# Gathering the first mixture's tokens in quarter rows, turning them on VectorE, and reading the newest activations last in its second products

## The chip, the cores and the metric

The kernel runs on one core of one Trainium2 chip. The metric is the device time of one execution in microseconds, the median of several runs. The engines are TensorE (PE; its weight loads are listed apart as PEld), VectorE (DVE), ScalarE (ACT), GpSimd (POOL) and SyncE (SP, which issues loads). Each works through its own instructions in order and waits for the others by semaphores.

## The reference

Three stages follow each other, all in float32. The first is a retention: per head a state that decays by gamma and takes in k times v, read by q. Its output is written as 1536 token rows of 512. The second is a mixture with hard routing: each token goes to the expert with the largest of 8 logits. The third is a mixture in which all 4 experts see every token, weighted by given probabilities.

```python
logits = x @ w_gate                       # first mixture: N=1536, D=512, E=8, F=1024
expert_idx = np.argmax(logits, axis=1)
# token i takes the next free place of its expert (capacity N // E * 2 = 384)
h = np.maximum(np.einsum('ecd,edf->ecf', disp, w1), 0.0)
y = np.einsum('ecf,efd->ecd', h, w2)
out[i] = gate_w[i] * y[expert_idx[i], pos[i]]
...
for e in range(E):                        # second mixture: E=4, F=1024
    h = np.maximum(x @ w1[e], 0.0)
    out += p[:, e:e + 1] * (h @ w2[e])
```

## The kernel before

**Precision.** A float32 matrix is split into a rounded high part and the remaining low part; a product is hi*hi + hi*lo + lo*hi. In the first mixture `pair` does this with two matmuls: the weights' high part against the tokens' high and low part side by side (448 columns), then the weights' low part against the tokens' high part (224). Splitting costs one ScalarE cast (L124) and one VectorE subtraction (L125) per weight unit of 128x1024 (`split_w`). The units of expert e are 8e to 8e+7: four for its first product (w1), four for its second (w2). SP loads a unit (L111) into one of four buffers, which is free again when the VectorE subtraction of an earlier unit has read it. `upto(u)` says how far the splits run ahead of the unit in use.

**Retention stage.** Twelve tiles of 128 tokens pass through matmuls; POOL scales v (`vg`, L230) and the outputs (`xT`, L316). `x_pe` turns a tile into token rows, ScalarE copies them to `xk` (L363), and an ACT-queue transfer writes them to `xd` in memory. VectorE works out each token's expert and rank, and matmuls collect into `slot_ps` which token stands at which place of which expert. `gidx` (L543) is the list of token numbers for 256 places of 8 experts. Expert 0's tokens are collected already transposed, by matmuls into `xt0` (`late`, `fetched`, L499 and L507), and split into `xet[0]` (L713, L717). Then all engines pass a branch (`overflow`, L580 and L581) that is not taken with these inputs.

**First mixture.** For each expert e: four groups c of the first product (L860, L863 with `xet`), each ending with ScalarE copy and Relu (L887, L888) and VectorE sum and low part (L889, L890) that give two of the eight blocks `hs`; then the tokens of expert e+1 are prepared by `prep_x`; then four output blocks d of the second product (L860, L863 with `h`), of which each two are summed into `x2` (L921, L922). `prep_x(e+1)` transposes the gathered rows with 8 TensorE matmuls against an identity (L701), splits them (L707, L708) and starts the gather for expert e+3 (`load_xe`, L570): two POOL instructions, each of 128 whole rows. Up to 224 places of an expert are used (`SM`). In between VectorE works off `tables` (pieces of the scatter tables), POOL scatters them (`scatter`, L841), and `combine_w` prepares weights for the second mixture.

**Second mixture.** All the rest, from `first_pair` on; it is TensorE's products nearly without a gap.

The order on each engine is the order in the code (the schedule is manual). What orders the preparation for the next expert is this end of the first product and the loop behind it:

```python
        if e + 1 < E1:
            prep_x(e + 1)
        if e == 3:
            for _ in pieces:
                pass
```

Of the kernel before, what the change touches and what calls it, by code (L numbers as in the profile page):

```python
# [37 lines left out]
NS = 2 * E2 * 4  # L38

C_D = 0  # L40
C_GK = C_D + P
C_IW = C_GK + NCH * 8
# [13 lines left out]
def tile_retention_moe_moe(ctx: ExitStack, tc, qkv, cst, gqt, a1, a2, b1, b2, out, cap):  # L56
# [31 lines left out]
    raws = {}  # L88
    ws = {}
# [10 lines left out]
    def wsrc(u):  # L100
        if isinstance(u, int):
            e, c = divmod(u, 8)
            return (a1 if c < 4 else a2)[e, c % 4]
        kind, n = u
        return (b1 if kind == "p" else b2)[n // 4 % E2, n % 4]
# [47 lines left out]
    gidx0 = pc.tile([P, SL // P], I32, name="gidx0")  # L153
    gidx = pc.tile([P, SL // P, E1], I32, name="gidx")
# [19 lines left out]
    pc.tile([P, 32], F32, name="edge")  # L174

    with ExitStack() as actx:
# [8 lines left out]
        zero = pa.tile([1, D], F32, name="zero")  # L185
        causal = cdec[:, C_D:C_GK].rearrange("p (o t) -> p o t", o=1).to_broadcast([P, 4, P])
        gk = cdec[:, C_GK:C_IW].rearrange("p (c h) -> p c h", c=NCH)
# [166 lines left out]
        def x_reduce(i):  # L354
            bks, part = xbs.pop(i)
            xk = xks[i]
            for g in range(2):
# [6 lines left out]
                    xk[:, g * 256:(g + 1) * 256].rearrange("p (q c) -> p q c", q=2), b3[:, :, 0:P]  # L364
# [72 lines left out]
        for it in range(NT):  # L437
# [105 lines left out]
        nc.vector.tensor_copy(gidx, slot_ps)  # L543
# [35 lines left out]
    def overflow():  # L579
        some = nc.values_load(nbi[0:1, 8:9], min_val=0, max_val=NB)  # L580
        with tc.If(some > 0, preferred_fallthrough_block=False), tc.tile_pool(name="pg", bufs=1, side="right") as pg:  # L581
# [23 lines left out]
            with tc.For_i(0, E1, 1) as e:  # L605
# [14 lines left out]
                with tc.For_i(0, blocks, 1) as j:  # L620
# [9 lines left out]
                    )  # L630
                    bk = bank("gt")
                    for k in range(KD):
                        nc.tensor.transpose(
                            bk[:, k * P:(k + 1) * P], xg[:, k * P:(k + 1) * P], ident
# [41 lines left out]
    xet = {}  # L676
    xet[0] = pw.tile([P, 2, 1024], F32R, tag="w", name="xet0").rearrange(
        "p a (b s t) -> p (a b) s t", b=2, s=2
    )[:, :, :, 0:SM]
# [12 lines left out]
    def prep_x(e):  # L692
        t = xe.pop(e)
        r = pe.tile([P, KD, 2, SL], F32R, tag="xet", name=f"xet{e}")[:, :, :, 0:SM]
        xet[e] = r
        t2 = duo(f"T{e}")
        bks = [t2[:, g] for g in range(2)]
        for b in range(2):
            for g in range(2):
                for q in range(2):  # L700
                    nc.tensor.transpose(  # L701
                        bks[g][:, (2 * q + b) * P:(2 * q + b + 1) * P],
                        t[:, b, (2 * g + q) * P:(2 * g + q + 1) * P], ident,
                    )
        t4 = t2.rearrange("p g (q t) -> p g q t", q=2)[:, :, :, 0:SM]
        hi, lo = (r[:, :, n].rearrange("p (g q) t -> p g q t", g=2) for n in range(2))
        nc.scalar.copy(hi, t4)  # L707
        nc.vector.tensor_tensor(out=lo, in0=t4, in1=hi.bitcast(F32), op=ALU.subtract)  # L708
# [3 lines left out]
    def hi0(g):  # L712
        nc.scalar.copy(xet[0][:, 2 * g:2 * g + 2, 0], xt0[g])  # L713

    def lo0(g):
        x = xet[0][:, 2 * g:2 * g + 2]
        nc.vector.tensor_tensor(  # L717
            out=x[:, :, 1], in0=xt0[g], in1=x[:, :, 0].bitcast(F32), op=ALU.subtract
        )

    hi0(0)
    lo0(0)
    hi0(1)
    lo0(1)
# [113 lines left out]

    def scatter(some):
# [28 lines left out]
    for e in range(E1):  # L868
        x = xet.pop(e)
        hs = []  # L870
        for c in range(4):
# [23 lines left out]
            if c != 2:  # L895
                upto(u)
# [408 lines left out]
```

## Time and profile before

| | |
|---|---|
| median of 3 runs | 744.47 us (744.29 to 746.27) |
| the profiled execution's own time | 744.18 us |
| its span, from first to last instruction | 742.4 us |
| mean granted TensorE clock | 0.997 |
| busy PE / PEld / DVE / ACT / POOL | 727.5 / 661.8 / 469.0 / 338.8 / 167.6 us |
| first mixture's first product to the second mixture's first | 68.13 to 237.22 us |

Times in the rows below are microseconds from the span's start unless marked ns. In a row of the time line the first number is the start and the second the length; "x8" is eight instructions shown as one row; a bracket at the end is the idle time of the engine ahead of the row and what ended it. Matmuls overlap: a new one starts before the last has ended, so their spacing counts, not their length.

### The profile page before, as it was taken

The numbers are of one execution on the slowest core, as the hardware profiler recorded it, in microseconds if no ns is written. First come the engines' busy times: TensorE is split into PE (matmuls) and PEld (weight loads), VectorE is DVE, ScalarE is ACT, GpSimd is POOL, SyncE is SP. The second block draws the span as 40 slices with busy tenths as digits, with TensorE's granted clock in tenths as the row PEclk, the third lists the DMA queues.
The fourth block names the chain that finished last, engine by engine and source line by source line (L and its number), as shares of the span: only waits on it lengthen the run. The fifth ranks groups of instructions, "written<-read, shape, count | busy, mean of one in ns | idle before, by whom it ended". The sixth has DMA issues, their size and how long they took to land.

```text
span 742.4 us, 11359 instructions
## 1 busy us (share of the span) xinstructions
PE 727.5 (98%) x4466; PEld 661.8 (89%) x4467; DVE 469.0 (63%) x769; ACT 338.8 (46%) x545; POOL 167.6 (23%) x158
## 2 busy tenths in 40 slices
PE   8998999999999999999999999999999999999996
PEld 5887999999998888899988999889998899988895
DVE  4888889887887935634754645773375454557334
ACT  2334666675665624334443335633445334453341
POOL 3543111222310011222222211213421121111103
PEclk9999999999999999999999999999999999999998
DMA  9985876687561122211113122112221212112002
GB/s 336 409 325 160 298 259 217 214 277 240 201 200 57 40 75 64 103 61 57 57 60 100 41 85 86 58 62 95 100 72 72 86 56 86 58 57 86 29 0 86
DMA packets 27642, 93.22 MB, mean 126 GB/s; under 512 B 3617, under 2 KB 3889, under 8 KB 27586
## 3 DMA queue, kind: packets, MB, share of 16 engines
q1 hardware_dynamic: 23042, 81.79, 31.9%
q0 software_dynamic: 2672, 7.44, 3.2%
q10 hardware_dynamic: 1872, 3.24, 1.1%
q8 instruction: 36, 0.59, 0.3%
q14 instruction: 20, 0.16, 0.1%
HBM read 86.11 MB, written 6.34 MB: 125 GB/s over the span
## 4 chain that ended last, share of the span: by engine, by line
PE 85%; DVE 5%; DMA 5%; ACT 1%; issue 1%; POOL 1%; POOLq 0%; SPq 0%; ACTq 0%; DVEq 0%
PE o L1111 35%; PE a L955 17%; PE m L860 11%; PE b L955 8%; PE m L863 5%; PE bb L955 5%; DMA kv<-qkv 2%; DVE w L125 2%; DMA qk<-qkv 1%; DMA xd<-xk 1%; DVE tsum L889 1%; PE O L301 1%; PE S L246 1%; DMA raw<-a 1%; PE T L701 1%
## 5 line engine op out<-in xcount | busy, mean ns | idle before, releaser
L1111 PE MATMUL o<-w,g_c 128*128 128x512 f32 x1152 | 267.4, 390 | 0.0
L1111 PEld LDWEIGHTS o<-w,g_c 128*128 128x128 f32 x1152 | 215.8, 188 | 43.8
L125 DVE TENSOR_TENSOR w<-raw,w 128x1024 fp32r<-128x1024 f32 x128 | 158.2, 1245 | 16.9 <-ACT w L124 16.7
L955 PE MATMUL a<-X,w 128*128 128x384 f32 x720 | 145.1, 336 | 0.0
L124 ACT CAST w<-raw 128x1024 fp32r<-128x1024 f32 x128 | 132.6, 1048 | 5.9 <-DMA raw<-a 4.2
L990 DVE TENSOR_TENSOR c<-b,c 128x384 f32<-128x384 f32 x30 | 16.7, 558 | 181.2 <-PE b L955 181.2
L955 PEld LDWEIGHTS a<-X,w 128*128 128x128 f32 x720 | 127.3, 188 | 2.6 <-DVE c L990 0.3
L139 POOL TENSOR_TENSOR t<-raw 128x512 f32<-128x512 f32 x28 | 38.8, 1386 | 375.2 <-DMA raw<-b 326.9
L986 ACT COPY c<-a 128x384 f32<-128x384 f32 x60 | 28.7, 479 | 196.4 <-PE a L955 196.4
L860 PE MATMUL m<-h,w 128*128 128x448 f32 x256 | 81.7, 378 | 1.7 <-DVE h L890 1.7
L860 PE MATMUL m<-xet,w 128*128 128x448 f32 x256 | 80.8, 375 | 0.9 <-DVE xet L717 0.9
L971 ACT ACTIVATE g_c<-c 128x384 fp32r<-128x384 f32 x96 | 50.4, 526 | 66.2 <-DVE c L990 64.9
L955 PE MATMUL b<-X,w 128*128 128x384 f32 x360 | 72.0, 334 | 0.0
L863 PE MATMUL m<-h,w 128*128 128x224 f32 x256 | 67.4, 263 | 0.0
L863 PE MATMUL m<-xet,w 128*128 128x224 f32 x256 | 67.4, 263 | 0.0
L955 PEld LDWEIGHTS b<-X,w 128*128 128x128 f32 x360 | 63.5, 188 | 0.0
L975 DVE SCALAR_TENSOR_TENSOR g_c<-c,g_c 128x384 fp32r<-128x384 f32 x96 | 52.9, 552 | 4.0
L860 PEld LDWEIGHTS m<-h,w 128*128 128x128 f32 x256 | 48.0, 187 | 6.1 <-ACT w L124 2.2
L860 PEld LDWEIGHTS m<-xet,w 128*128 128x128 f32 x256 | 48.0, 187 | 4.7 <-PEq L581 1.0
L863 PEld LDWEIGHTS m<-h,w 128*128 128x128 f32 x256 | 48.8, 191 | 0.0
L863 PEld LDWEIGHTS m<-xet,w 128*128 128x128 f32 x256 | 48.8, 190 | 0.0
L955 PE MATMUL bb<-X,w 128*128 128x384 f32 x204 | 41.3, 339 | 0.1
(148 smaller groups left out, 747.1 us busy)
## 6 DMA issues: line engine op xcount, KB each, us to landing
raw<-a SPq DMA_DIRECT2D x64, 512.0 KB, 4.3
raw<-b SPq DMA_DIRECT2D x64, 512.0 KB, 3.5
qk<-qkv SPq DMA_DIRECT2D x12, 512.0 KB, 8.4
kv<-qkv SPq DMA_DIRECT2D x12, 512.0 KB, 8.3
xd<-xk ACTq DMA_DIRECT2D x12, 256.0 KB, 6.6
gqs<-gqt SPq DMA_DIRECT2D x6, 256.0 KB, 7.7
iw<-cst SPq DMA_DIRECT2D x1, 272.0 KB
xe<-xd,gidx POOLq DMA_INDIRECT x16, 4.2
```

Source lines behind the costliest of these rows:

```text
L124: nc.scalar.copy(w[:, 0], r)
L125: nc.vector.tensor_tensor(out=w[:, 1], in0=r, in1=w[:, 0].bitcast(F32), op=ALU.subtract)
L139: eng.tensor_tensor(out=c[:, 0:2], in0=b[:, 2:4], in1=b[:, 1:3], op=sub)
L246: nc.tensor.matmul(out=bks[j][:, cols], lhsT=qk[r, 1, cols], rhs=qk[r, 0, cols], start=True, stop=True,)
L860: nc.tensor.matmul(out=b2, lhsT=w[0], rhs=x, start=first, stop=last, skip_group_check=True)
L863: nc.tensor.matmul(out=b2[:, 0], lhsT=w[1], rhs=x[:, 0], start=False, stop=last, skip_group_check=True)
L955: nc.tensor.matmul(out=bk[:, 0:HT], lhsT=w[:, sw, k], rhs=x[:, sx, k], start=(first and m == 0), stop=(m == len(steps) - 1), skip_group_ch ...
L971: nc.scalar.activation(out=h2[:, 0], in_=src, func=AF.Relu)
L975: nc.vector.scalar_tensor_tensor(out=h2[:, 1], in0=src, scalar=0.0, in1=h2[:, 0].bitcast(F32), op0=ALU.max, op1=ALU.subtract,)
L986: nc.scalar.copy(t, bk[:, 0:HT])
L990: nc.vector.tensor_tensor(out=t, in0=bk[:, 0:HT], in1=t, op=ALU.add)
L1111: nc.tensor.matmul(out=bk, lhsT=h2[:, sh, cols], rhs=w[:, sw, k], start=(q == 0 and m == 0 and (n, t) not in begun), stop=(m == 2), skip_g ...
```

## The change

The tokens of experts 1 to 7 are gathered in quarter rows. `xd` is read as four times as many rows of 128 floats, and one gather instruction fetches 32 tokens with their four quarters, one quarter to each group of 32 partitions. So an expert takes 7 gather instructions (224 / 32) where it took 2. The rows of `xd` are stored with their columns permuted, so that VectorE's transpose of 32x32 squares (one instruction, `turn_x`) gives the transposed tokens; the 8 TensorE transposes are gone. The index list is made by repeating each token number four times over partitions with seven small matmuls against `rep` (filled by POOL in the third retention tile), times four plus the quarter's number (`gidx`, now one VectorE instruction from PSUM). Expert 0's tokens, which are not gathered this way, keep the permuted column order, and its w1 comes in that order as a separate input `a0`.

The order of work: `turn_x(e+1)` stands in the third group (c = 2) of expert e, the high part behind the fourth group, the low part behind the second product's first pair of output blocks. For expert 1 the turn stands in expert 0's d = 1, the high part behind that place's splits, and the low part behind the split in d = 2. `xet[0]` is made ahead of the overflow branch, and `gidx` behind it but also ahead of the branch. Output blocks d = 0 and 1 are issued together: six of the eight steps of each, then the four steps that read the two newest blocks of h. Some splits and the two `combine_w` around expert 7 are placed anew, the table pieces come two per block in experts 1 to 3 instead of three in 1 and 2, and the scatters run in experts 4 to 6, four per expert, into views that are declared disjoint.

```diff
-def tile_retention_moe_moe(ctx, tc, qkv, cst, gqt, a1, a2, b1, b2, out, cap):
+def tile_retention_moe_moe(ctx, tc, qkv, cst, gqt, a0, a1, a2, b1, b2, out, cap):
...
+        rep = pa.tile([P, 4, P], F16, name="rep")
...
                 nc.scalar.copy(
-                    xk[:, g * 256:(g + 1) * 256].rearrange("p (q c) -> p q c", q=2), b3[:, :, 0:P]
+                    xk.rearrange("p (b k c) -> p k b c", b=4, k=KD)[:, 2 * g:2 * g + 2],
+                    b3[:, :, 0:P].rearrange("p q (b c) -> p q b c", b=4),
                 )
...
                 nc.vector.tensor_copy(ident, iw[:, 0, 0:P])
+                for q in range(4):
+                    nc.gpsimd.tensor_copy(
+                        rep[:, q].rearrange("p (b c) -> p b c", b=4),
+                        iw[:, 0:1, 32 * q:32 * q + 32].to_broadcast([P, 4, 32]),
+                    )
...
         split_w(1)
-        nc.vector.tensor_copy(gidx, slot_ps)
+        nc.vector.tensor_copy(rows, slot_ps.rearrange("p b e -> p (b e)"))
+        rps = bank("rows")[:, 0:NB4 * E1]
+        for b in range(NB4):
+            nc.tensor.matmul(
+                out=rps[:, b * E1:(b + 1) * E1], lhsT=rep[:, b % 4],
+                rhs=rows[:, b // 4 * E1:(b // 4 + 1) * E1],
+                start=(b == 0), stop=True, skip_group_check=True,
+            )
+        xet[0] = ...
+        for g in range(2):
+            x = xet[0][:, 2 * g:2 * g + 2]
+            nc.scalar.copy(x[:, :, 0], xt0[g])
+            nc.vector.tensor_tensor(
+                out=x[:, :, 1], in0=xt0[g], in1=x[:, :, 0].bitcast(F32), op=ALU.subtract
+            )
+        nc.vector.tensor_scalar(
+            out=gidx.rearrange("p b e -> p (b e)"), in0=rps, scalar1=4.0,
+            scalar2=cdec[:, C_PB:C_PB + 1], op0=ALU.mult, op1=ALU.add,
+        )
...
+    xq = xd.rearrange("n (q c) -> (n q) c", q=4)
+
     def load_xe(e):
-        t = pe.tile([P, SL // P, D], F32, tag="xe", name=f"xe{e}")
-        for b in range(SL // P):
+        t = pe.tile([P, 1024], F32, tag="xe", name=f"xe{e}")[:, 0:NB4 * P].rearrange(
+            "p (b c) -> p b c", b=NB4
+        )
+        for b in range(NB4):
             nc.gpsimd.indirect_dma_start(
-                out=t[:, b], out_offset=None, in_=xd,
+                out=t[:, b], out_offset=None, in_=xq,
                 in_offset=bass.IndirectOffsetOnAxis(ap=gidx[:, b, e:e + 1], axis=0),
             )
...
-    def prep_x(e):
-        t = xe.pop(e)
+    def turn_x(e):
+        t = xe.pop(e).rearrange("p b (k c) -> p b k c", k=KD)
+        x = pe.tile([P, 1024], F32, tag="xT", name=f"xT{e}", bufs=1)[:, 0:KD * SM].rearrange(
+            "p (k t) -> p k t", k=KD
+        )
+        nc.vector.transpose(x.rearrange("p k (b c) -> p b k c", b=NB4), t)
...
+    def hi_x(e):
+        nc.scalar.copy(xet[e][:, :, 0], turned[e])
+
+    def lo_x(e):
+        r = xet[e]
         nc.vector.tensor_tensor(
+            out=r[:, :, 1], in0=turned.pop(e), in1=r[:, :, 0].bitcast(F32), op=ALU.subtract
+        )
...
+    last = {W0 - 8: 0, W0 - 5: 1, W0 - 4: 2, W0 - 3: 3, W0 - 2: 3, W0 - 1: 3}
+
     def upto(u):
-        ahead = DEPTH + sum(u >= v for v in (5, 7, 29, 31)) - sum(u >= v for v in (W0 - 6, W0 - 5))
-        while nsplit[0] <= min(u + ahead, W0 + 3):
+        ahead = DEPTH + sum(u >= v for v in (5, 7, 29, 31))
+        to = W0 + last[u] if u in last else min(u + ahead, W0 - 1)
+        while nsplit[0] <= to:
...
-            if c != 2:
+            if c == 2 and 0 < e < E1 - 1:
+                turn_x(e + 1)
+            if u == W0 - 7:
+                combine_w(1, nc.vector)
+            elif c != 2:
                 upto(u)
-        if e + 1 < E1:
-            prep_x(e + 1)
+        if 0 < e < E1 - 1:
+            hi_x(e + 1)
...
-            bk = bk2[:, d % 2]
-            for k in range(KF):
-                pair(bk, [w[:, s, k] for s in range(2)], hs[k], k == 0, k == KF - 1)
+                w2 = [ws[u + n].rearrange("p s (k d) -> p s k d", k=KF) for n in range(2)]
+                order = [(n, k) for n in range(2) for k in range(KF)]
+                if d == 0:
+                    order.sort(key=lambda m: m[1] >= KF - 2)
+                for n, k in order:
+                    pair(
+                        bk2[:, n], [w2[n][:, s, k] for s in range(2)], hs[k],
+                        k == 0, k == KF - 1,
+                    )
...
+            if e == 0 and d == 1:
+                turn_x(1)
+            if d == 0 and 0 < e < E1 - 1:
+                lo_x(e + 1)
             upto(u)
-            if W0 - 11 < u < W0 - 8:
-                combine_w(u - W0 + 10, nc.vector)
-            if e in (1, 2):
-                for _ in range(3):
+            if e == 0 and d == 1:
+                hi_x(1)
+            if e == 0 and d == 2:
+                lo_x(1)
+            if u == W0 - 9:
+                combine_w(0, nc.vector)
+            if e in (1, 2, 3):
+                for _ in range(2):
                     next(pieces, None)
```

## Rows read from the trace of the kernel before

**Rows 1.** The page, the chain that ended last by engine.

```profile
PE 85%; DVE 5%; DMA 5%; ACT 1%; issue 1%; POOL 1%; POOLq 0%; SPq 0%; ACTq 0%; DVEq 0%
```

**Rows 2.** Windows: stretch, length, busy (count) PE, PEld, DVE, ACT, POOL; clock, DMA share, GB/s.

```profile
68.13:89.13 21.00, 21.00 (x136) 20.06 (x137) 18.16 (x27) 14.23 (x20) 7.79 (x6) 1.00 0.83 270
89.13:110.51 21.38, 21.16 (x138) 20.00 (x137) 18.48 (x26) 14.77 (x22) 2.19 (x2) 1.00 0.80 270
110.51:131.44 20.93, 20.93 (x139) 20.00 (x137) 19.06 (x33) 13.44 (x19) 3.03 (x3) 1.00 0.72 225
...
152.37:173.48 21.11, 21.11 (x139) 20.01 (x137) 18.63 (x21) 14.38 (x20) 6.98 (x6) 1.00 0.86 281
...
215.33:237.22 21.89, 20.37 (x130) 19.12 (x129) 17.29 (x24) 11.37 (x17) 0.00 (x0) 1.00 0.37 121
```

**Rows 3.** Time line of TensorE, expert 1: first product's pairs, transposes, second product.

```profile
89.13 0.37 PE L860 MATMUL m<-xet,w 128*128 128x448 f32 x1
...
98.84 0.38 PE L860 MATMUL m<-xet,w 128*128 128x448 f32 x1
...
99.17 1.04 PE L701 MATMUL T<-ident,xe 128*128 128x128 f32 x8
99.96 0.45 PE L860 MATMUL m<-h,w 128*128 128x448 f32 x1
...
102.30 0.44 PE L860 MATMUL m<-h,w 128*128 128x448 f32 x1 [0.22 <-DVE h L890]
```

**Rows 4.** Time line of TensorE, expert 7, around its wait in the second product.

```profile
227.22 0.27 PE L863 MATMUL m<-h,w 128*128 128x224 f32 x1
229.01 0.44 PE L860 MATMUL m<-h,w 128*128 128x448 f32 x1 [1.52 <-DVE h L890]
```

**Rows 5.** Time line of POOL in the retention stage.

```profile
22.31 1.07 POOL L230 TENSOR_TENSOR vg<-kv,cdec 128x512 f32<-128x512 f32 x1 [0.94 <-DMA kv<-qkv]
```

**Rows 6.** Time line of TensorE at the start of the first mixture.

```profile
65.26 2.00 PE L507 MATMUL T0x<-ident,xe 128*128 128x128 f32 x16
68.13 0.44 PE L860 MATMUL m<-xet,w 128*128 128x448 f32 x1 [0.86 <-DVE xet L717]
```

**Rows 7.** Time line of VectorE in the same place.

```profile
67.87 0.62 DVE L717 TENSOR_TENSOR xet<-T0x,xet 128x448 fp32r<-128x448 f32 x1 [0.26 <-ACT xet L713]
...
69.50 1.23 DVE L125 TENSOR_TENSOR w<-raw,w 128x1024 fp32r<-128x1024 f32 x1
```

**Rows 8.** Time line of POOL, first gathers; then the tile xe, landing of its DMAs.

```profile
68.21 0.94 POOL L570 DMA_INDIRECT xe<-xd,gidx  x1 [5.79 <-ACT xet L713]
69.46 0.95 POOL L570 DMA_INDIRECT xe<-xd,gidx  x1 [0.30 <-issue]
70.71 1.97 POOL L570 DMA_INDIRECT xe<-xd,gidx  x1 [0.30 <-issue]
72.98 1.09 POOL L570 DMA_INDIRECT xe<-xd,gidx  x1 [0.30 <-issue]
...
DMA to landing us min/median/max: 3.3/4.2/7.3
```

**Rows 9.** Groups of VectorE's instructions by shape, retention stage: busy us, mean ns | idle.

```profile
L418 DVE TENSOR_SCALAR at<-kc,ranks 128x256 f16<-128x256 f32 x12 | 4.1, 352 | 0.0
```

**Rows 10.** Time line of VectorE, expert 0's second product.

```profile
82.91 1.08 DVE L708 TENSOR_TENSOR xet<-T,xet 128x896 fp32r<-128x896 f32 x1
...
85.83 2.36 DVE L125 TENSOR_TENSOR w<-raw,w 128x1024 fp32r<-128x1024 f32 x2 [0.17 <-ACT w L124]
89.43 1.23 DVE L125 TENSOR_TENSOR w<-raw,w 128x1024 fp32r<-128x1024 f32 x1 [1.24 <-ACT w L124]
```

**Rows 11.** Time line of SP: the load of unit 11 is issued.

```profile
83.03 0.58 SPq L111 DMA_DIRECT2D raw<-a  x1
```

**Rows 12.** Time line of ScalarE: the cast of unit 11.

```profile
88.35 1.05 ACT L124 CAST w<-raw 128x1024 fp32r<-128x1024 f32 x1 [1.60 <-DMA raw<-a]
```

**Rows 13.** The tile raw from 60 to 110 us, landing of its loads.

```profile
DMA to landing us min/median/max: 3.6/4.4/6.4
```

More of the change, by code (lines that the diff above doesn't have):

```diff
@@ L38 @@
 NS = 2 * E2 * 4
+NB4 = SM // 32
 C_D = 0
 C_GK = C_D + P
-C_IW = C_GK + NCH * 8
+C_PB = C_GK + NCH * 8
+C_IW = C_PB + 16
 C_U = C_IW + XW
@@ L55, in tile_retention_moe_moe @@
 @with_exitstack
-def tile_retention_moe_moe(ctx: ExitStack, tc, qkv, cst, gqt, a1, a2, b1, b2, out, cap):
+def tile_retention_moe_moe(ctx: ExitStack, tc, qkv, cst, gqt, a0, a1, a2, b1, b2, out, cap):
     nc = tc.nc
@@ L152, in tile_retention_moe_moe @@
     ident = pc.tile([P, P], F32, name="ident")
-    gidx0 = pc.tile([P, SL // P], I32, name="gidx0")
-    gidx = pc.tile([P, SL // P, E1], I32, name="gidx")
+    gidx = pc.tile([P, NB4, E1], I32, name="gidx")
     cum = pc.tile([P, NT + 1, 8], F16, name="cum")
@@ L185, in tile_retention_moe_moe @@
         zero = pa.tile([1, D], F32, name="zero")
+        rep = pa.tile([P, 4, P], F16, name="rep")
+        rows = pa.tile([P, 2 * SL // P * E1], F16, name="rows")[:, 0:SL // P * E1]
+        gidx0 = pa.tile([P, 16], I32, name="gidx0")[:, 0:SL // P]
         causal = cdec[:, C_D:C_GK].rearrange("p (o t) -> p o t", o=1).to_broadcast([P, 4, P])
-        gk = cdec[:, C_GK:C_IW].rearrange("p (c h) -> p c h", c=NCH)
+        gk = cdec[:, C_GK:C_PB].rearrange("p (c h) -> p c h", c=NCH)
         st = [pa.tile([P, KD, HD], F32, name=f"st{b}") for b in range(2)]
@@ L630, in overflow @@
                     )
+                    xn = pg.tile([P, D], F32, name="gxn")
+                    nc.vector.tensor_copy(
+                        xn.rearrange("p (k b c) -> p b k c", k=KD, b=4),
+                        xg.rearrange("p (b k c) -> p b k c", b=4, k=KD),
+                    )
                     bk = bank("gt")
@@ L690, in tile_retention_moe_moe @@
     xe = {1: load_xe(1)}
-    def prep_x(e):
-        t = xe.pop(e)
+    def turn_x(e):
[4 more added lines that the diff above has]
+        nc.vector.transpose(x.rearrange("p k (b c) -> p b k c", b=NB4), t)
         r = pe.tile([P, KD, 2, SL], F32R, tag="xet", name=f"xet{e}")[:, :, :, 0:SM]
         xet[e] = r
[L696 to L708, printed above, removed]
+        turned[e] = x
         if e + 2 < E1:
             xe[e + 2] = load_xe(e + 2)
[L712 to L716, printed above, removed]
+    turned = {}
+    def hi_x(e):
+        nc.scalar.copy(xet[e][:, :, 0], turned[e])
+    def lo_x(e):
+        r = xet[e]
         nc.vector.tensor_tensor(
-            out=x[:, :, 1], in0=xt0[g], in1=x[:, :, 0].bitcast(F32), op=ALU.subtract
+            out=r[:, :, 1], in0=turned.pop(e), in1=r[:, :, 0].bitcast(F32), op=ALU.subtract
         )
[L721 to L724, printed above, removed]
     offsets()
@@ L841, in scatter @@
             nc.gpsimd.indirect_dma_start(
-                out=td, out_offset=bass.IndirectOffsetOnAxis(ap=posi[:, i:i + 1], axis=0),
+                out=tds[i], out_offset=bass.IndirectOffsetOnAxis(ap=posi[:, i:i + 1], axis=0),
                 in_=tt[:, i], in_offset=None,
@@ L894, in tile_retention_moe_moe @@
             del ws[u]
-            if c != 2:
+            if c == 2 and 0 < e < E1 - 1:
[3 more added lines that the diff above has]
+            elif c != 2:
                 upto(u)
-        if e + 1 < E1:
-            prep_x(e + 1)
-        if e == 3:
+        if 0 < e < E1 - 1:
+            hi_x(e + 1)
+        if e == 4:
             for _ in pieces:
                 pass
-        if 3 <= e < E1 - 1:
-            scatter(range(3 * e - 9, 3 * e - 6))
+        if 4 <= e < E1 - 1:
+            scatter(range(4 * e - 16, 4 * e - 12))
         rv = nc.vector.value_load(offi[0:1, e:e + 1], min_val=0, max_val=N)
@@ L1263, in pack @@
     ).reshape(P, NT * E2)
+    turned = np.arange(D).reshape(KD, 4, 32).transpose(1, 0, 2).reshape(D)
+    w1 = np.asarray(inputs["moe_w1"])[:, rows]
     def w_in(a):
@@ L1282, in pack @@
         "gqt": gqt,
-        "a1": w_in(np.asarray(inputs["moe_w1"])[:, rows]),
+        "a0": w_in(w1[0:1, turned]),
+        "a1": w_in(w1),
         "a2": a2,
```

18 lines of the change are left out of this document (10 added, 8 removed).

## The prediction

> **What bounds the kernel now.** I read the page first, then the windows cut at each expert's first matmul, then the time lines of the five engines. The chain that ended last is 85% TensorE [rows 1]: where TensorE has no gap, only less TensorE work or a removed gap shortens the run. The second mixture's products are not touched, so I count what the diff does to their start.
>
> The first mixture runs from TensorE's 68.13 to 237.22 us. The windows give 21.00, 21.38, 20.93, 21.11 and 21.89 us for experts 0, 1, 2, 4 and 7 [rows 2]; 3, 5 and 6 last as long as 2. What would a pure stream of products last? From the first to the last of one first product's 32 pairs (448 columns, then 224) are 31 steps over 98.84 - 89.13 = 9.71 us, 0.313 us a pair [rows 3]. An expert has 64 pairs: 20.05 us, eight 160.4. The stage lasts 169.1, so 8.7 us are not products:
> - Transposes: eight 128x128 ones between an expert's two products. The first starts at 99.17, the second product at 99.96 [rows 3]: 0.8 us, seven times. The windows say 0.9 with the change of stream.
> - A wait in expert 1 for the newest h (0.22 us idle, about 0.4 beyond the pair spacing) [rows 3], and the same in expert 7, 1.52 us idle, 229.01 - 227.22 = 1.79 between two pairs instead of 0.10 [rows 4]. The second product's first output block reaches the two newest h after six pairs.
>
> **What the change takes away.** All 56 TensorE transposes go: 7 x 0.87 = 6.1 us, by 20.93 - 20.05 of an ordinary expert. The second product now does six pairs of d=0, six of d=1, then the four with the newest h. Six pairs more are 1.88 us of cover; against that 0.8 us of transposes no longer cover anything. Net +1.08 us where there were transposes (expert 1 lacked 0.4), +1.88 in expert 7 (lacked 1.7). Expert 7 is close, but its VectorE also loses two jobs ahead of the last h: one of two combinations and one split are moved later or earlier. If that did not suffice, up to 1.7 us of its wait would stay. I let both waits go, and with 0.2 us of expert 4 the stage could fall to 160.4: at most -8.7 us.
>
> **What it adds, by place.**
> *Attention.* The POOL copies that fill rep come in the third tile; vg, four times as wide, takes 1.07 us there and POOL had waited 0.94 us for a load before it [rows 5], so at about 0.26 us each they are nearly covered: 0, at worst 1 us. Zero for the ScalarE copies with a permuted output (same elements, same engine; loads bound this stage, and only the last tile's two copies lack cover), the wider constants, the disjoint scatter views (they only take POOL waits away) and the later td scatter.
>
> *Before expert 0.* TensorE ends the fetched tokens at 67.26, then passes the overflow branch, and starts at 68.13 [rows 6]. Now seven 8-column matmuls come first, and gidx is computed on VectorE after both low parts (end 68.49 [rows 7]), and only then VectorE branches. I take +0.5 us for TensorE (0 if the branch overlaps, 1.0 if the bank that gidx reads holds the first product up): start 68.6. The splits that started at 69.50 [rows 7] start some 0.6 later, with TensorE some 2 us away from needing the first.
>
> *Gathers.* Seven instructions of 128 quarter rows in place of two of whole rows, so POOL issues 49 for 14. Two starts are 1.25 us apart when undisturbed; the one at 70.71 lasts 1.97 us and the next starts 2.27 later [rows 8]. The three intervals there average 1.59, so an expert takes 11.1 of POOL's 20 us, of which 3.03 are busy now in expert 2 [rows 2]: room. For expert 1, starting at about 68.9, behind gidx, the seventh starts at 78.4 and lands 4.2 later (3.3 to 7.3 [rows 8]): 82.6, bounds 79.7 (1.25, 3.3) and 89.8 (2.27, 7.3). Bytes do not grow (224 rows for 256).
>
> *VectorE transposes.* One per expert, 128x896, one SBUF input. No row shows one. The nearest one-input row is 256 columns in 0.35 us [rows 9], the nearest of that width 1.08 with two inputs [rows 10]. I take 1.1 us; 0.6 if it runs twice as fast, 2.2 if half. The low part stays at 1 us. VectorE is busy 18.48 us in expert 1 [rows 2], but the sum overstates: two splits last 2.36, not twice 1.23 [rows 10], so each of 26 instructions hides some 0.1 in the next, and 15.9 remain. With the transpose 17.0 of 20.05: it fits, and hides behind products.
> The Trainium skill, VectorE: DVE Perf Modes, The three transpose paths, gives 311 ns for a 128x128 bf16 transpose on VectorE; seven would be an estimate of 2.2 us, my upper end, and by it the sum below worsens by about 1 us in expert 0 alone.
>
> *Expert 1's tokens, where a wait appears.* For experts 2 to 7 the turn comes a product early. Expert 1's does not: its turn follows the d=1 sum of expert 0, then the splits of units 9 and 10, the high part on ScalarE, the split of unit 11, and behind that the low part. Before, everything was ready at 83.99 [rows 10]. Unit 11's split starts at 89.43, since its raw load was issued at 83.03, after unit 7's split, and ScalarE could only cast it at 88.35, having waited 1.60 us for it [rows 10, 11, 12]. Those same steps stand now, 0.4 later by the start: split 89.8, 1.13 to the next start, low part 90.9 to 91.9. TensorE is through with expert 0 at 68.6 + 20.05 = 88.65: a wait of 3.3 us. That load took 5.3 us; were it the fastest of its stretch, 3.6 [rows 13], the wait is 1.6; with the gather landing at 89.8, turn, three splits and low part (1.1 + 3.4 + 1.0) end at 95.3: 6.7. At the median, 4.4, it is 2.4. I keep 3.3, because this very load ran beside a gather and will again, and the gather's likely landing is covered. Behind the wait VectorE has d=3's sum and two splits, ready before expert 1's second group needs them.
>
> **The sum.** Stage 169.1 to 160.4: -8.7. Start +0.5, wait +3.3: **-4.9 us**. The profiled execution is 744.18 (span 742.4): 739.3. The median of the runs shown is 744.47, 0.29 above it: 739.6. With the bounds of the wait -6.6 to -1.5.
>
> **Rivals.**
> *The wait does not form* (split 11 earlier): -8.2, 736.3. For it: raw loads have landed in 3.6 us [rows 13]. Against it: the 1.60 us that ScalarE waited, and in-order VectorE.
> *Late gather.* Landing after 86.5, each us costs one: at 89.8 it is -1.5, 743. For it: the 1.97 us row, when a split ran beside. This is what the Trainium skill, SBUF — State Buffer, Who interferes with whom, says: a VectorE instruction with two SBUF inputs shuts out a GpSimd one that reads SBUF. The trace agrees in that long row, and shows two of 0.94 and 0.95 [rows 8].
> *VectorE binds.* Above 4.1 us a transpose, its 15.9 us pass 20.05. At 6 each of six experts costs 1.9: -4.9 + 11.4 = +6.5, 751. Against it: seventeen times what 256 columns take [rows 9].
> *Slower: POOL binds.* Seven issues pass 20.05 us above 2.87 us apiece. At 3.2, each of six experts costs 2.3 us more and expert 1 waits 9: -8.2 + 9 + 14, 759. It needs gathers beyond the slowest spacing seen (2.27), all of them; the 1.25 us rows speak against it. It is slower than before from about 2.95 on.
> *Nothing comes back:* TensorE's gaps reappear as waits for splits, 744.5; against that, experts 2 and later have no gap but the transposes [rows 2].
>
> **From cases to numbers.** Forecast 0.55, no wait 0.18, late gather 0.12, VectorE 0.03, POOL 0.05, nothing 0.07. The bound for a measurable change is 0.3%, 2.2 us. Faster: the first two and two thirds of the late gather: 0.81. Same: the rest of it and nothing: 0.11. Slower: VectorE and POOL: 0.08. The range runs from the no-wait case, with 0.4 below it, to the middle of the late gathers: 735.9 to 742.4, which leaves out about 0.2. The forecast's own range is 738.6 to 741.
>
> **What would show it.** No transposes on TensorE; windows of experts 2 to 7 at 20.05 to 20.2; one gap ahead of expert 1's first product, released by VectorE's low part, near 88.7 to 92; no gap six pairs into a second product; POOL's gathers 1.25 to 2.3 apart; a transpose row of about 1.1. Wrong would be: a gap at every expert's start (POOL or VectorE late each time), a first product later than 69.2, a transpose above 2.5.

## The result, and the profile after

The changed kernel takes 747.42 us, the median of 22 executions (743.94 to 757.57); the kernel before, beside it, 745.14 (743.84 to 746.27, 22 executions). The ratio is 1.0053, 95% interval 1.0027 to 1.0079: slower by half a percent, where 739.6 was predicted. (The ratio compares means and leaves out the two executions more than 1.5% above the kernel's fastest, so it is not the ratio of the medians, 1.003.) The changed kernel is also less steady: the kernel before stays within 2.4 us, while twelve executions of the changed one lie at 743.9 to 747.4 and ten at 751.4 to 757.6. The profiled execution took 747.41 (span 745.7, mean granted clock 0.994).

Windows of the changed kernel, cut where first products start: retention; experts 0, 1, 2, 4, 5 and 7; second mixture up to the last matmul; what follows it. Columns as in [rows 2].

```profile
0.00:70.15 70.15, 63.36 (x898) 53.04 (x899) 48.35 (x195) 22.98 (x62) 28.79 (x34) 1.00 0.81 310
70.15:94.54 24.39, 20.28 (x129) 19.12 (x129) 20.15 (x29) 15.67 (x22) 19.05 (x16) 1.00 0.63 213
94.54:116.26 21.72, 21.72 (x129) 20.61 (x129) 18.38 (x25) 13.33 (x19) 14.02 (x11) 0.92 0.70 243
116.26:136.31 20.05, 20.05 (x131) 19.12 (x129) 18.40 (x28) 13.46 (x19) 9.27 (x8) 1.00 0.71 236
156.37:177.38 21.01, 20.28 (x131) 19.12 (x129) 19.45 (x27) 14.86 (x21) 8.93 (x7) 1.00 0.79 255
177.38:197.43 20.05, 20.05 (x131) 19.12 (x129) 18.15 (x21) 13.70 (x20) 16.09 (x14) 1.00 0.75 242
217.49:237.54 20.05, 20.05 (x131) 19.12 (x129) 17.28 (x25) 11.36 (x17) 0.00 (x0) 1.00 0.42 138
237.54:735.83 498.29, 497.80 (x2498) 450.04 (x2496) 276.83 (x386) 207.34 (x329) 100.46 (x98) 1.00 0.20 67
735.83:745.70 9.87, 0.38 (x2) 0.00 (x0) 0.75 (x1) 0.00 (x0) 2.08 (x3) 0.75 0.20 81
```

The same two last windows of the kernel before:

```profile
237.22:735.45 498.23, 497.77 (x2498) 450.33 (x2496) 276.84 (x386) 207.24 (x329) 100.41 (x98) 1.00 0.20 67
735.45:742.40 6.95, 0.38 (x2) 0.00 (x0) 0.75 (x1) 0.00 (x0) 2.07 (x3) 0.67 0.28 115
```

What the reader is to see: an ordinary expert lasts 20.05 us for 20.93 before [rows 2], and expert 7 20.05 for 21.89. So transposes and waits for h did go, expert 4's excepted. But the stage, 167.39 us, is only 1.70 shorter. Four things ate the gain: expert 0 (24.39, with the gap at its end), expert 1 at a granted clock of 0.92 (21.72), expert 4 (21.01), and, outside the stage, a first product 2.02 us later (70.15 for 68.13) and a tail behind the last matmul of 9.87 for 6.95. Balance: -1.70 + 2.02 + 2.92 + 0.06 (second mixture) = +3.3, the difference of the spans.

The gap ahead of expert 1, in TensorE's time line: the last matmul of output blocks 0 and 1, the last of blocks 2 and 3, the first of expert 1. Then ScalarE, then VectorE, same place.

```profile
85.15 0.26 PE L895 MATMUL m<-h,w 128*128 128x224 f32 x1
...
90.17 0.26 PE L895 MATMUL m<-h,w 128*128 128x224 f32 x1
94.53 0.44 PE L892 MATMUL m<-xet,w 128*128 128x448 f32 x1 [4.11 <-ACT w L129]
```
```profile
81.30 2.94 ACT L129 CAST w<-raw 128x1024 fp32r<-128x1024 f32 x3
87.68 0.53 ACT L962 COPY tsum<-m 128x448 f32<-128x448 f32 x1 [3.44 <-remote]
88.11 2.00 ACT L129 CAST w<-raw 128x1024 fp32r<-128x1024 f32 x2
90.03 0.94 ACT L744 CAST xet<-xT 128x896 fp32r<-128x896 f32 x1
90.87 1.04 ACT L129 CAST w<-raw 128x1024 fp32r<-128x1024 f32 x1
92.96 0.53 ACT L962 COPY tsum<-m 128x448 f32<-128x448 f32 x1 [1.05 <-remote]
```
```profile
88.30 0.62 DVE L963 TENSOR_TENSOR x<-m,tsum 128x448 f32 x1 [2.10 <-issue]
88.85 1.10 DVE L734 STREAM_TRANSPOSE xT<-xe 128x896 f32<-128x896 f32 x1
89.87 3.45 DVE L130 TENSOR_TENSOR w<-raw,w 128x1024 fp32r<-128x1024 f32 x3
93.24 1.08 DVE L748 TENSOR_TENSOR xet<-xT,xet 128x896 fp32r<-128x896 f32 x1
```

The chain (turn, three splits, low part) is the predicted one, and the transpose takes the predicted 1.10 us. But it starts late for a reason that the prediction had not named. ScalarE's copy reads blocks 0 and 1, whose last matmul ends by its row at 85.41. The copy starts at 87.68, 2.27 us later, and ScalarE had been idle for 3.44. The next such copy starts 2.5 us behind its matmuls (90.43 to 92.96); ScalarE was casting until 91.91 and then idle for 1.05. "remote" means that the profile finds no instruction that ended just then. Elsewhere this copy follows the matmul's end by 0.04 us. TensorE's row names ScalarE's cast as what ended its wait, but that cast ended at 91.91; the low part, which ends at 94.32, is what the start at 94.53 fits.

Behind the gap the granted clock falls to half, 1.2 GHz, for 3.41 us:

```profile
94.54:95.68 1.14, 1.14 (x7) 1.09 (x8) 1.14 (x2) 1.02 (x1) 0.85 (x1) 1.00 0.95 287
95.68:99.09 3.41, 3.41 (x14) 3.15 (x13) 1.45 (x2) 0.53 (x3) 2.79 (x3) 0.50 0.99 378
```

TensorE never waits in it; 1.7 us are lost. The kernel before has no such stretch ahead of its tail.

GpSimd's gathers, the first three and the group of all:

```profile
70.92 0.94 POOL L606 DMA_INDIRECT xe<-xd,gidx  x1 [7.59 <-DVE offb L579]
72.16 1.75 POOL L606 DMA_INDIRECT xe<-xd,gidx  x1 [0.30 <-issue]
74.21 0.94 POOL L606 DMA_INDIRECT xe<-xd,gidx  x1 [0.30 <-issue]
...
L606 POOL DMA_INDIRECT xe<-xd,gidx x49 | 63.8, 1303 | 54.1 <-DVE xT L734 33.1 <-issue 13.1 <-DVE offb L579 7.6
```

They stand 1.25 to 2.3 us apart, as predicted; the long one lies beside VectorE's splits. Nothing waits for their landing here.

### The profile page after: what moved, and what is told of

It reads as the page before. It is cut to its first block, busy times and chain, and to the rows that moved or that the text cites. A ratio compares the mean times of both kernels' runs of the same rounds, so it can differ in the third digit from the quotient of the medians.

```text
span 745.7 us, 11329 instructions
## 1 busy us (share of the span) xinstructions
PE 724.1 (97%) x4417; PEld 657.6 (88%) x4418; DVE 473.5 (64%) x777; ACT 340.0 (46%) x545; POOL 211.4 (28%) x197
## 4 chain that ended last, share of the span: by engine, by line
PE 82%; DVE 2%; ACT 2%; issue 1%; DMA 1%; another core or an unknown queue 1%; POOL 1%; ACTq 0%; POOLq 0%; SPq 0%; DVEq 0%
PE o L1160 34%; PE a L1004 17%; PE m L892 12%; PE b L1004 8%; PE m L895 6%; PE bb L1004 5%; ACT w L129 1%; DMA raw<-a 1%; DVE w L130 1%; POOL out_dram L1172 1%; PE ab L1004 0%; DVE x L797 0%; DVE tsum L921 0%; DVE X L810 0%
## 5 line engine op out<-in xcount | busy, mean ns | idle before, releaser
L892 PE MATMUL m<-xet,w 128*128 128x448 f32 x256 | 82.4, 380 | 5.6 <-ACT w L129 4.1
L606 POOL DMA_INDIRECT xe<-xd,gidx x49 | 63.8, 1303 | 54.1 <-DVE xT L734 33.1
L892 PEld LDWEIGHTS m<-xet,w 128*128 128x128 f32 x256 | 48.8, 191 | 9.7 <-ACT w L129 4.4
L895 PEld LDWEIGHTS m<-xet,w 128*128 128x128 f32 x256 | 49.6, 194 | 0.0
```

The costliest lines, as they stand in the source:

```text
L606: nc.gpsimd.indirect_dma_start(out=t[:, b], out_offset=None, in_=xq, in_offset=bass.IndirectOffsetOnAxis(ap=gidx[:, b, e:e + 1], axis=0),)
L892: nc.tensor.matmul(out=b2, lhsT=w[0], rhs=x, start=first, stop=last, skip_group_check=True)
L895: nc.tensor.matmul(out=b2[:, 0], lhsT=w[1], rhs=x[:, 0], start=False, stop=last, skip_group_check=True)
```

## The experiments

"Before" below is the kernel before, timed on the same chip.

**1. The same kernel again.** No edit.

> The changed kernel once more, for a second trace. In the first, TensorE stood 4.3 us ahead of expert 1's first product, and the next 3.4 us ran at half clock, which cost 1.7 us more. If the wait for expert 1's tokens is what takes the gain back, this trace has a gap of 3 to 9 us in the same place, with a stretch at half clock behind it, and nothing of the kind elsewhere; a longer execution has a longer gap or a longer stretch there. If the gathers are the cause (rival 1), POOL's issues are over 2.3 us apart or experts 2 to 7 have gaps too. If the later start is the cause (rival 2), the first product starts at 70 us again and the gap is small.

762.66 us, one execution. TensorE stood still for 5.34 us inside expert 0's second product, 3.25 ahead of expert 1, 1.79 in expert 4 and 3.81 in expert 5, and the clock was at half for four stretches. So the gap of the profiled run is one of several that come and go. The first and the last have its mark: ScalarE waits for a completion of TensorE (the news that a group of matmuls has ended) that arrives long after the row of its last matmul, here 6.4 us (80.81 to 87.20) and 4.9 us (195.99 to 200.86):

```profile
87.20 0.53 ACT L919 COPY tsum<-m 128x448 f32<-128x448 f32 x1 [7.88 <-remote]
200.86 0.53 ACT L919 COPY tsum<-m 128x448 f32<-128x448 f32 x1 [6.35 <-remote]
```

The other two don't: ahead of expert 1 TensorE waits for the low part, which ends at 100.43, and in expert 4 for an h of VectorE, which had been held up by a raw load (ScalarE waits 1.76 us for it).

**2. Expert 1's parts straight behind its turn.**

```diff
             if e == 0 and d == 1:
                 turn_x(1)
+                hi_x(1)
+                lo_x(1)
```
(and out of their old places)

> High and low part of expert 1's tokens stand straight behind the turn, ahead of the splits of units 9, 10 and 11. If the wait sits in that order, the low part ends some 2.4 us earlier (two or three splits less ahead of it), the gap ahead of expert 1 falls from 4.3 to about 2 us, the stretch at half clock shrinks or goes, and the median falls by 3 to 4 us, to 743.5 to 744.5, below the kernel before by 1. If late gathers hold the turn (rival 1), the gap stays at 4 us and the time at 747.

744.22 us (742.76 to 756.12), 1.0006 of before (0.9977 to 1.0034): the median is as expected, but four of twelve executions are above 752. The profiled execution is one of these (756.12). It shows no gap ahead of expert 1 and 20.1 us for expert 0, but 7.42 us in expert 5's second product, behind a completion that is 9.8 us late (184.86 to 194.64). The predicted wait can be ordered away; the irregular stalls stay.

**3. Expert 1 by whole rows and TensorE, the others as changed.**

```diff
-    xe = {1: load_xe(1)}
+    xe = {1: load_x1()}
...
+        if e == 0:
+            prep_x1()
```
(`load_x1` is two whole-row gathers, `prep_x1` eight TensorE transposes)

> Expert 1 alone is served as before: two gathers of whole rows and eight TensorE transposes behind expert 0's first product (its w1 in the permuted order); experts 2 to 7 as changed. If the wait for expert 1 is the whole loss, no gap is left: expert 0 takes 20.9 us and seven experts 20.05, 161.3 us for the stage against 169.1, and with a start some 1 us later the time is 6 to 7 us below the kernel before, 738 to 739. If the gathers of experts 2 to 7 cost (rival 1), there are gaps at their starts and the time stays above 742. If the later start is the loss (rival 2), it is 741.

745.31 us (743.53 to 757.77), 1.0023 (0.9991 to 1.0055). A miss: 738 to 739 was expected. Late tokens of expert 1 aren't the main loss; four of twelve executions are still above 751.

**4. The kernel before with the new order of the second product alone.**

```diff
+                if d == 0:
+                    order.sort(key=lambda m: m[1] >= KF - 2)
```

> The kernel before with nothing but the new order of d = 0 and 1. By the prediction's sum the waits for the newest h in experts 1 (0.4) and 7 (1.7) go, and no more: 2.1 us below the kernel before, 743. If the new order itself slows TensorE (rival), expert windows without these waits grow above 20.93, and the time is 745 or more.

742.44 us (742.05 to 743.82), ratio 0.9968 (0.9957 to 0.9980): faster than both kernels, by 2.7 us where the sum had 2.1 for the order. Expert 7 lasts 20.06 us for 21.89:

```profile
68.36:89.37 21.01, 21.01 (x137) 20.07 (x137) 18.15 (x27) 13.93 (x20) 7.83 (x6) 1.00 0.80 266
89.37:110.30 20.93, 20.93 (x139) 20.00 (x137) 18.23 (x26) 14.99 (x22) 2.32 (x2) 1.00 0.85 273
...
214.93:234.99 20.06, 20.06 (x131) 19.13 (x129) 17.23 (x24) 11.40 (x17) 0.00 (x0) 1.00 0.37 124
```

**5. The new `last` and `combine_w` places besides.** To experiment 4 they are added.

> The kernel before, with the new order in the second products and the new order of the splits at the end of the last expert; gathers, transposes and scatters as before. Both theories: no stall, tail 7.0 us. The order alone gave 742.4; the splits that now come earlier ahead of the second mixture can give 0 to 1.5 more: 741.0 to 742.5.

742.55 us (741.96 to 743.44), 0.9963 (0.9950 to 0.9976): they add nothing.

So the loss lies in the gathers, the turn or the scatters. **6. Scatters of the changed kernel wait for each other again.**

```diff
-                out=tds[i], out_offset=...
+                out=td, out_offset=...
```

> The kernel after, with one edit: the twelve indirect DMAs that scatter the second mixture's table write the whole table again, so that each waits for the one before it. Theory of the bursts: TensorE's matmuls end on time, but its completion reaches ScalarE late while GpSimd issues indirect DMAs back to back. Then the stalls of 4 to 7 us in expert 5, where the twelve scatters follow seven gathers without a pause, are gone, the burst of fourteen gathers in expert 0 still can stall, and the median falls to 743 to 745 with fewer executions above 750. Theory of the turn: VectorE's transpose, in its place between two halves of the first product, holds the engines up whenever a gather is late. Then this edit changes nothing: 744 to 747, stalls in expert 5 as before.

747.42 us (745.82 to 751.9), 1.003 (1.002 to 1.0041). The median didn't fall to 743 to 745, but one execution of eight is above 750, where ten of 22 were. (The code gives four scatters to each of experts 4 to 6; GpSimd, which waits for nothing there, ran all twelve in one go in the changed kernel, from 181.76 us on.) The profile has no stall in expert 5, which says little, since the changed kernel's first profile has none there either; ahead of expert 1 it has one of 7 us. ScalarE and TensorE there:

```profile
91.16 0.53 ACT L960 COPY tsum<-m 128x448 f32<-128x448 f32 x1 [6.46 <-remote]
```
```profile
90.40 0.37 PE L890 MATMUL m<-h,w 128*128 128x448 f32 x1
91.17 0.34 PE L893 MATMUL m<-h,w 128*128 128x224 f32 x1 [0.40 <-issue]
98.00 0.71 PE L890 MATMUL m<-xet,w 128*128 128x448 f32 x1 [6.49 <-issue]
```

The copy at 91.16 reads matmuls whose rows end at 85.9; their semaphore is recorded at 91.14, that of the next 32 matmuls at 92.87. 32 matmuls take 5.0 us, so they can't all have run in those 1.73: it is the news of the first that came late, 5.3 us behind its row. TensorE itself went on for 31 matmuls with their weight loads; the 32nd, at 91.17, is the first that stands 0.77 us behind the one before it instead of 0.2.

**7. The kernel before with disjoint scatters.** The edit of 6, the other way round.

> The kernel before, with one edit: its twelve scatters write views that are told to be disjoint, as in the kernel after, so that none waits for another; they stay three to an expert. Theory of the bursts: its bursts are of three scatters and two gathers, so stalls are rare or small, and the time stays within 744 to 746. Theory of the turn: the same. A time above 747, or a stall of over 2 us in expert 4 or 5, would put the cause on the scatters alone.

745.74 us (745.17 to 747.45), 1.0006 (0.9997 to 1.0015): nothing, as both theories wanted. The scatters alone are not it.

**8. The kernel before with five unused gathers per expert.**

```diff
+        for b in range(5):
+            x = pe.tile([P, P], F32, tag=f"idle{b}", name=f"idle{e}_{b}", bufs=1)
+            nc.gpsimd.indirect_dma_start(
+                out=x, out_offset=None, in_=xq,
+                in_offset=bass.IndirectOffsetOnAxis(ap=gidx[:, b % 2, e:e + 1], axis=0),
+            )
```

> The kernel before, with five more gathers of 128 quarter rows for each of experts 1 to 7, into buffers that nobody reads, so seven gathers to an expert as in the kernel after, and 51 indirect DMAs in all; the transposes stay on TensorE and nothing waits for the new gathers but GpSimd. Theory of the bursts: stalls in which all engines wait for TensorE's completion appear here too, in expert 0 or 1 above all, 2 to 6 us in some executions, and the tail behind the last matmul grows from 7.0 to 9.9 us, as in the kernel after: 748 to 752. Theory of the turn: no stall, and at most the tail: 745 to 748. If neither the tail nor a stall comes: 744.5 to 745.5.

758.41 us (753.63 to 763.66), 1.0179 (1.0136 to 1.0222), though nothing reads what they fetch. ScalarE in expert 0, one copy per group of the first product:

```profile
70.72 0.53 ACT L895 COPY tsum<-m 128x448 f32<-128x448 f32 x1 [1.14 <-PE m L871]
...
74.50 0.54 ACT L895 COPY tsum<-m 128x448 f32<-128x448 f32 x1 [1.86 <-PE m L871]
...
78.26 0.53 ACT L895 COPY tsum<-m 128x448 f32<-128x448 f32 x1 [1.84 <-PE m L871]
...
84.06 0.53 ACT L895 COPY tsum<-m 128x448 f32<-128x448 f32 x1 [4.82 <-remote]
```

The groups' copies should stand 2.5 us apart, as the products do; they stand 3.8, 3.8 and 5.8 apart. This kernel has no turn: the theory that VectorE's turn waits for a late gather falls. The tail is 9.80 us, as in the changed kernel.

**9 to 12. Where the unused gathers must stand.** The same edit with 25 for experts 3 to 7 (`range(5 if e > 2 else 0)`), ten for experts 1 and 2, 35 for experts 3 to 7, 20 for experts 1 to 4.

> The kernel before with the five unused gathers for experts 3 to 7 alone, 25 of them; at the start, where GpSimd would issue the gathers of experts 1 and 2 in one run, nothing is added. Theory of the bursts: the tail grows by 25 times 0.084 us, from 7.0 to 9.1; runs of seven gathers stall seldom; 746.5 to 748. If each gather costs something wherever it stands: 25 of 35 of what all of them cost, about 754.

> The kernel before with the five unused gathers for experts 1 and 2 alone, ten of them, all in GpSimd's first run. If the cost is that of the long run at the start: tail 7.0 + 10 x 0.084 = 7.8 us, late completions and a stall in expert 0 or 1, and 753 to 757 (the 758.4 with all 35 less the 3.2 that the other 25 cost). If the cost needs all 35: 745.5 to 748.

> The kernel before with seven unused gathers for each of experts 3 to 7, 35 in all, none for experts 1 and 2. If the number in the whole kernel decides: late completions in expert 0 or 1 again, 753 to 763. If the place decides: no late completion, tail 9.9 us, 749 to 750.

> The kernel before with five unused gathers for each of experts 1 to 4, 20 in all. If the number in the whole kernel decides and 25 were too few: no late completion, tail 8.7 us, 747 to 748.5. If a long run at the start with more behind it decides: late completions and 752 to 760.

| experiment | added gathers | median, us | lowest and highest | ratio to before |
|---|---|---|---|---|
| 9 | 25, experts 3 to 7 | 748.42 | 747.91, 748.81 | 1.0043 (1.0030 to 1.0056) |
| 10 | 10, experts 1 and 2 | 746.48 | 745.70, 747.37 | 1.0029 (1.0017 to 1.0040) |
| 11 | 35, experts 3 to 7 | 752.64 | 752.27, 756.01 | 1.0118 (1.0099 to 1.0137) |
| 12 | 20, experts 1 to 4 | 758.01 | 753.68, 760.49 | 1.0162 (1.0135 to 1.0190) |

Only the last shows the large stall: expert 0 lasts 35.2 us for 21.0. If the long run at the start were the cause, 10 should have shown it too; in the profile of 11 the loss beyond the tail is waits for h in experts 1, 4 and 5, without a late completion. In the profile of 12 TensorE itself crawls; the last matmul of expert 0's first product and the eight transposes that follow it, and in the last line those of the kernel with ten:

```profile
79.10 0.35 PE L871 MATMUL m<-xet,w 128*128 128x224 f32 x1 [0.38 <-issue]
80.49 0.32 PE L709 MATMUL T<-ident,xe 128*128 128x128 f32 x1 [1.04 <-issue]
81.92 0.37 PE L709 MATMUL T<-ident,xe 128*128 128x128 f32 x1 [1.11 <-issue]
83.32 0.37 PE L709 MATMUL T<-ident,xe 128*128 128x128 f32 x1 [1.03 <-issue]
...
87.57 0.37 PE L709 MATMUL T<-ident,xe 128*128 128x128 f32 x1 [0.25 <-issue]
```
```profile
78.28 1.04 PE L709 MATMUL T<-ident,xe 128*128 128x128 f32 x8
```

"issue" is idle time in which the engine waits for nothing that the profile shows. Until 88 us the two kernels have the same instructions, and one crawls there while the other doesn't; the times, which don't overlap, say the same of the other executions. So the long run of gathers at the start isn't sufficient, and the number is not the measure either (35 late: 7.6 us, 20: 13.0). Ahead of the crawl news is late here too: a group whose matmuls end at 73.5 is copied at 79.09, after 31 more matmuls. A late fetch of TensorE's own instructions is unlikely: from 71 to 93 us this trace has no packet on the instruction queues.

**13 to 15. The same places without an indirect DMA.** Five plain loads of the same size by GpSimd (`nc.gpsimd.dma_start`), five by SyncE (`nc.sync.dma_start`), five copies of 128x384 on GpSimd.

> The kernel before with five plain loads of 128 rows of 512 B behind the gathers of each of experts 1 to 7, issued by GpSimd; no index is read. If any DMA that GpSimd issues lengthens the tail, it grows from 7.0 to 9.9 us, and if the runs of them make TensorE's completions late, stalls appear in expert 0 or 1: 752 to 760, as with the unused gathers. If only indirect ones do: tail 7.0 us and no late completion; what is left is GpSimd's time, as with the copies: 746 to 750.

> The kernel before with the same amount of unused traffic, but not by GpSimd: five plain loads of 128 rows of 512 B for each of experts 1 to 7, issued by SyncE between its weight loads. Theory of the bursts (what hurts is GpSimd's issuing): no stall, tail 7.0 us, 744.5 to 747, the rise being later weight loads. Theory of the traffic (what hurts is the transfers of small rows): stalls and a time as with the unused gathers, above 750.

> The kernel before with five copies of 128 x 384 numbers on GpSimd, some 0.9 us each, behind the gathers of each of experts 1 to 7, at the places where the other kernel had five unused gathers; no DMA is added. Theory of the bursts (indirect DMAs in a row): no stall over 2 us, tail 7.0 us, 744.5 to 746.5. If it is enough that GpSimd is busy: a stall of some us in expert 0 or 1 and a time above 748.

749.47 us, 1.0069 (1.0056 to 1.0083), for the plain loads by GpSimd; 749.61, 1.0047 (1.0029 to 1.0065), for those by SyncE; 749.13, 1.0049 (1.0035 to 1.0063), for the copies. Each costs 4 to 5 us (2.9 of the first is tail), against my theory that GpSimd's bursts alone hurt; but in none of the three profiles does a completion come late. Kernel 13 moves the same 28763 packets and 95.52 MB as the one of experiment 8, so neither packets nor bytes as such make the stalls. The loss beside the tail stands mostly in expert 1, where weights come late (and, in 14 and 15, the clock then falls to half for 3.4 and 6.8 us); ScalarE in the kernel with the copies:

```profile
91.61 1.05 ACT L124 CAST w<-raw 128x1024 fp32r<-128x1024 f32 x1 [4.15 <-DMA raw<-a]
```

**16. Runs of at most seven.** One buffer for gathered rows, so that an expert's gathers wait for the turn before; turn and both parts behind the first pair of output blocks; scatters as in 6.

> The kernel after with its bursts of indirect DMAs cut: one buffer for gathered rows in place of two, so that an expert's seven gathers start only when the tokens of the expert before have been turned; turn, high part and low part stand together behind the first half of the second product in every expert; the scatters wait for one another again and come behind the gathers. The same gathers and transposes are made. Theory of the bursts: no stall is left; the first product starts at 69 to 70.6, seven experts of 20.05 us and the last of about 20 bring the stage's end to 230 to 231, the last matmul to 728.5 to 729.5, and with a tail of 9.9 us the time is 740 to 743, with executions close together. If a burst of seven is enough to stall, or the cause is the quarter-row gather as such: stalls as before, 744 to 750.

745.81 us, 745.20 to 746.87 in eleven executions, 1.0010 of before (1.0001 to 1.0019). The spread is gone, as the theory of the bursts wants. The level isn't 740 to 743: with the turn in its new place TensorE waits for h and for the low part in experts 1 and 4 (windows of 22.48 and 22.47 us).

**17. Experts 1 and 2 by whole rows, 3 to 7 as changed, scatters as in 6.** The edit of 3 for one more expert.

> The kernel after with experts 1 and 2 fetched by whole rows and turned on TensorE, as in the kernel before, so that GpSimd's first run is four gathers and not fourteen, and with scatters that wait for one another; experts 3 to 7 as in the kernel after. Theory of the bursts: no stall over 2 us; three windows of about 21 us and five of 20.05 to 20.2 from a start at 69 to 70 end the stage at 232 to 233, the last matmul at 730.5 to 731.5, and with 25 more indirect DMAs than before a tail of 9.1 us: 741 to 743, executions close together. If single runs of seven still stall: 744 to 748.

743.41 us (742.45 to 744.28), 0.9976 (0.9967 to 0.9985): steady, no large stall, at the edge of the 741 to 743 expected; a little faster than before, not faster than experiment 4.

**18. The row products in another bank.** `bank("rows", "u")`.

> The kernel after, with the PSUM bank of the row products moved to one that the first two products of the stage don't use. If the read of that bank by VectorE, for the table of gather rows, held the first product up, TensorE's gap of 1.62 us ahead of it falls to 0.6 to 1.1 us and the first product starts at 68.2 to 69.7. If the gap stays 1.62 us, another wait ends last there. The time of this one execution is too spread to read: 742 to 760.

745.28 us, one execution. TensorE is idle for 1.46 us ahead of the first product, as before the edit, and starts just behind the instruction that makes `gidx`. The bank was the wrong suspect, or not the only one. The first product's row names VectorE's sequencer at the overflow branch as what ended the wait (L617 here), as do those of all eight profiles with the gather table; no edit tested that.

```profile
69.06 0.44 PE L892 MATMUL m<-xet,w 128*128 128x448 f32 x1 [1.46 <-DVEq L617]
```

The profile is of use for more: but for the bank it is the changed kernel, and no completion is late in it. Ahead of expert 1 it shows the predicted wait. ScalarE waits for the raw load of the second of the three splits, the low part ends at 92.44, and TensorE starts at 92.64; expert 0 lasts 23.58 us, 3.53 above 20.05:

```profile
87.34 1.05 ACT L129 CAST w<-raw 128x1024 fp32r<-128x1024 f32 x1 [1.50 <-DMA raw<-a]
91.35 1.09 DVE L748 TENSOR_TENSOR xet<-xT,xet 128x896 fp32r<-128x896 f32 x1
92.64 0.44 PE L892 MATMUL m<-xet,w 128*128 128x448 f32 x1 [3.30 <-ACT w L129]
```

**The tail, over all of them.** From the start of the last matmul to the span's end:

| added GpSimd DMAs | kernels | tail, us |
|---|---|---|
| 0 | before, 4, 15 (copies), 14 (SyncE's loads) | 6.95, 7.02, 6.91, 7.05 |
| 10, 20, 25, 25 | 10, 12, 9, 17 | 7.83, 8.87, 9.05, 9.00 |
| 35 | after, 8, 11, 13 (plain loads) | 9.87, 9.80, 9.80, 9.83 |

2.9 us for 35 is 0.083 us for each added DMA that GpSimd issues, indirect or plain, read or not, hundreds of microseconds earlier.

## Why the prediction was wrong

*The stage, -8.7.* Right in size where the stage runs freely: 20.05 us in experts 2, 5 and 7 of the profiled run. The new order holds (experiment 4: -2.6 us, 1.8 of it in expert 7), and so does the transpose's 1.1.

*The gathers: failed.* The step read "so an expert takes 11.1 of POOL's 20 us, of which 3.03 are busy now in expert 2 [rows 2]: room". Spacing and room were right, but 35 more DMAs were priced by GpSimd's time and landing alone. They cost 2.9 us in the tail, which the sum did not have at all, and they bring stalls of TensorE, which none of the rivals had: "late gather" and "POOL binds" are about waiting for gathers, and unused gathers do the same harm (experiment 8). The rival of the late gather was drawn from the Trainium skill, SBUF — State Buffer, Who interferes with whom: a VectorE instruction with two SBUF inputs contends with a GpSimd one that reads SBUF. The trace agrees in that the long gathers lie beside splits (1.75 us for 0.94), but in the profiled run nothing waits for one.

*The wait, +3.3.* Right in size and mechanism where no completion is late (experiment 18: 3.5, with ScalarE waiting for a raw load, if of another unit). In the profiled run it measured 4.3 (expert 0's 24.39 less 20.05), inside 1.6 to 6.7, but by luck: there the chain started 2.27 us late behind a completion, and ScalarE waited for no raw load in it.

*The clock: missing.* 1.7 us in expert 1 behind the gap, in the profiled run and in experiment 18; a gap was counted as if the products behind it ran at 2.4 GHz.

*Expert 4* waits 0.96 us for h, where the sum had let its 0.2 go.

*Start, +0.5.* In eight profiles with the gather table the first product starts at 68.7 to 70.6 us, in twelve without it at 68.0 to 68.7; mean 69.5 against 68.2. So +1.2, above the bound of 1.0; in the profiled run 2.0, of which the retention stage, ending about 1 us later there, is part.

For the profiled run: tail 2.9, start 1.5 more, clock 1.7, wait 1.0 more, expert 4 1.0: 8.1 of the 8.2 us between -4.9 and +3.3. In experiment 18, whose span is 1.1 us above before's, 6.0 are to be explained without any stall: tail 2.9 and clock 1.7, then start, second mixture and expert 4 with 0.4 each and the wait with 0.2. So tail and clock alone take 4.6 of the 4.9 back; the stalls make the long executions.

Shown is that added GpSimd DMAs alone, in the old kernel, reproduce tail and stalls. Fewer gathers in GpSimd's first run went with steady executions (16 and 17, in both of which the scatters wait too). Only argued is how: TensorE behaves as if its finished instructions were taken off late, so that news of them arrives late and, some 31 matmuls on, it can't issue (6 and 12). Which arrangement triggers it stays open: kernels 10 and 12 differ only behind the place where one stalls. Whether the recording of the executions has a part in it, no run here tells.

## What to carry to other kernels

Work moved to a free engine as more DMAs is not free because that engine has room: put unused copies of those DMAs into the old kernel first, which takes ten lines and here would have shown the loss without the change (and overstated it: 12.9 us). Read the end of the span too, and count a gap with the half clock behind it. When a change has several parts, time the cheapest alone: the order of the second product gave 2.7 us, more than any kernel with the new gathers.

## What the runs showed of the hardware

- The end of the kernel grew by 0.083 us for every DMA that GpSimd issued beyond before's, for 10 to 35 of them, as the table's kernels show; 35 loads by SyncE added 0.1 us in all.
- TensorE's completions can reach other engines 2.3 us (the profiled run) to 9.8 us (experiment 2) after the rows of its matmuls, with ScalarE and VectorE idle meanwhile; and TensorE can issue matmuls 1.4 us apart (experiment 12) that stand 0.1 apart in a kernel with the same instructions up to there (10).
- At or behind such gaps the granted clock was at half for stretches of 3.4 us (the profiled run), 6.8 (experiment 8), 10.2 (6) and 17.1 us (12, from the crawl on).
- Beside copies on GpSimd some of VectorE's splits took 1.52 us for 1.22 (experiment 15; the median split is unchanged).
